# Two-stage attention and two dense layers on one Trainium2 core: a list order made at build time, weight conversion spread over the loads, and half-height matmuls in place of zero-padded ones

## Chip, cores and metric

The kernel runs on 1 core of one Trainium2 chip. The metric is the device time of one execution in microseconds (us); lower is better. The engines are named as in the profile: PE (matmul), PEld (its weight loads, which overlap PE), DVE (vector), ACT (scalar), POOL (GpSimd), SP (which only issues DMAs here).

## The reference, cut to what matters

```python
batch, n_heads, seq, head_dim = 8, 8, 576, 64        # q, k, v; p has 32 rows per head
def sm_attn(qq, kk, vv):
    a = softmax(qq @ kk.T / 8)                         # with the row maximum taken off
    return a @ vv
p_packed = sm_attn(p, k, v)                            # 32 x 64 per head
attn = sm_attn(q, p_packed, p_packed)                  # 576 x 64 per head
x = attn as [4608, 512]
h = x @ w_in1                                          # [4608, 2048]
g = (a0 + a1 h + a2 h^2 + a3 h^3) / (1 + |b0| |h| + |b1| h^2 + 1e-6)
x = g @ w_out1                                         # [4608, 512]
h = x @ w_in2
out = (h * cos(h)) @ w_out2
```

The four weight matrices come as 64-bit floats and are turned into 32-bit ones on the chip from their two 32-bit words.

## The kernel before

**Attention.** A unit is one batch with four of its eight heads: 16 units. For each unit SP loads p, k, q and v (`load`), PE transposes p, k and q, PE computes the packed scores (`scores`, 0), DVE and ACT do their softmax, PE transposes the exponentials (`turn_exp`), and `pack` multiplies them with v: 6 column blocks of 96 rows times 4 heads, 24 matmuls. The packed rows are transposed (`turned`, `by_parity`), stored to DRAM (`keep_pack`) and used for the second scores. The second softmax runs on DVE, POOL and ACT (`turn2` to `turn_back`), and its 32x576 per head go to DRAM (`keep_attn`).

A head has only 64 contraction rows. `by_parity` writes each head's 64 rows into a 128-row operand whose other 64 rows are zero, and one matmul always uses all 128 rows of the array. `m_load` and `m_prod` (line 249) do the same for the first layer: the attention output of a batch is a product of the second softmax with packed rows, so `m_prod` multiplies the packed rows with `w_in1` first. A batch needs 8 such products, each [128, 512] from 4 matmuls of 32 output rows; `m_hi` (ACT, L259) and `m_lo` (DVE, L263) split each into two 32-bit parts of lower precision, whose sum is the value. There are 64 products in all.

**First layer.** 16 half batches of 288 rows times 8 pairs of 128 hidden columns make 128 items. An item is a `front` (L326, 12 matmuls of 288 columns into a PSUM tile `h`), an epilogue, and a `back` (L363, 24 matmuls of 288 columns, which add onto four accumulators). The epilogue has on ACT `absolute`, `lin`, `slope`, `rsqrt`, `square`, `upper`; on POOL `denom` (L437); on DVE `cubic` twice (L423, L425, they read `h` in PSUM) and four steps whose operands all lie in SBUF: `over` twice (L447), `ratio` (L451), `lower` (L479, which makes `gl`).

**Second layer.** 9 chunks of 512 rows times 16 column blocks make 144 items with a `front` (L342) and a `back` (L363) of 12 matmuls each, 512 columns wide.

**Weights.** A tile of 128x512 64-bit values is loaded (`w_load`), ACT makes two parts (`w_exp` L131, `w_low` L136), DVE joins them (`w_abs` L146, `w_join` L163), and `w_split` or `keep_hi`/`keep_lo` split the result (ACT, POOL). There are 64 tiles, 16 for each matrix, and two landing buffers (`raw`).

**Order.** Each engine runs its instructions in the order in which the program issues them. That order is written out by hand: every step has a time in units of items (`plan`, `plan1`, `plan2`, `begins`, `starts`, `weight_steps`, `MOVED`), and the steps are issued sorted by it. In the first layer it has a fixed period:

```python
plan1 = (
    (0.000, front), (0.437, absolute), (0.583, lin), (0.620, slope), (0.626, cubic, 0), (0.735, denom),
    (0.882, cubic, 1), (1.753, rsqrt), (1.895, square), (2.041, over, 1), (2.097, over, 0), (2.388, ratio),
    (3.033, upper), (3.268, lower), (4.074, back, 2), (4.275, back, 1), (4.724, back, 3), (4.790, back, 0),
)
```

## Time and profile before

| what | value |
|---|---|
| median of 3 runs (range) | 1717.53 us (1717.34 to 1721.29) |
| the profiled execution, its own time | 1716.86 us |
| its span, first to last instruction | 1715.1 us |
| PE, DVE, ACT, POOL busy | 1622.7, 1371.0, 1072.2, 347.0 us |
| mean granted clock of PE | 0.983 of 2.4 GHz |
| moved by DMA | 120.77 MB |

A busy time is the sum of the stretches in which an engine runs something. An engine that is busy for almost all of a stage bounds it; the stages here have different bounds, so the tables below go by stage.

### The profile page before, as it was taken

What the parts mean: (1) busy time and instruction counts of PE and PEld (TensorE: products, weight loads), DVE (VectorE), ACT (ScalarE), POOL (GpSimd) and SP (SyncE); (2) the same over time, 40 slices, a digit from 0 to 9 for tenths busy, and PEclk for the clock granted to TensorE, in tenths of its full rate; (3) what the DMA queues carried; (4) which work ended last, traced back from release to release, by engine and by line L of the source; (5) the groups of instructions that cost most, each with busy time, mean ns of one, the idle gap of its engine ahead of it and who ended that gap; (6) DMA issues with size and microseconds to landing.
All of it is one profiled execution on the core that took longest, in us unless ns stands there. A gap on an engine that the chain in (4) does not pass through costs nothing.

```text
span 1715.1 us, 26803 instructions
## 1 busy us (share of the span) xinstructions
PE 1622.7 (95%) x10272; PEld 1354.7 (79%) x10272; DVE 1371.0 (80%) x2057; ACT 1072.2 (63%) x1770; POOL 347.0 (20%) x252
## 2 busy tenths in 40 slices
PE   5877779999999999999999999999999999999997
PEld 3554668989898988898998778888888888888886
DVE  4678999999999999999999976666676667666765
ACT  6766888888898888888886643434333333343432
POOL 1334543424343433333322200000000000000000
PEclk9888889999999999999999999999999999999999
DMA  9998321111211121111353210101010101010001
GB/s 293 273 264 249 111 83 54 48 51 49 71 49 46 49 71 49 47 37 34 117 182 101 86 44 7 44 7 44 6 38 13 37 13 37 13 33 17 22 4 25
DMA packets 78881, 120.77 MB, mean 70 GB/s; under 512 B 14752, under 2 KB 54688, under 8 KB 78752
## 3 DMA queue, kind: packets, MB, share of 16 engines
q1 hardware_dynamic: 78752, 119.05, 23.7%
q8 instruction: 81, 1.33, 0.3%
q14 instruction: 48, 0.39, 0.1%
HBM read 85.99 MB, written 33.03 MB: 69 GB/s over the span
## 4 chain that ended last, share of the span: by engine, by line
PE 73%; DVE 11%; DMA 6%; ACT 5%; issue 4%; SPq 0%; POOL 0%; DVEq 0%; ACTq 0%
PE acc L363 38%; PE h L342 21%; PE h L326 9%; DMA raw<-in_moe_w_in_dram 3%; PE m L249 3%; DMA raw<-in_moe_w_out_dram 2%; DVE T L447 2%; DVE T L451 2%; DVE gl L479 1%; DVE Q L447 1%; DVE w L163 1%; DVE w L146 1%; DVE T L423 1%; ACT g L131 1%; ACT w L136 1%
## 5 line engine op out<-in xcount | busy, mean ns | idle before, releaser
L363 PE MATMUL acc<-gh,wo 128*128 128x288 f32 x2048 | 419.9, 299 | 0.0
L363 PEld LDWEIGHTS acc<-gh,wo 128*128 128x128 f32 x2048 | 328.6, 188 | 50.5 <-issue 20.0
L363 PE MATMUL acc<-wo,gh 128*128 128x512 f32 x1152 | 359.5, 393 | 0.0
L363 PE MATMUL acc<-gl,wo 128*128 128x288 f32 x1024 | 303.2, 296 | 1.0 <-DVE gl L479 1.0
L437 POOL TENSOR_TENSOR Q<-Q,V 128x576 f32<-128x576 f32 x128 | 199.2, 1556 | 402.8 <-ACT Q L431 287.4
L463 ACT ACTIVATE Y<-Y,cst 128x512 f32<-128x512 f32 x144 | 104.4, 725 | 253.8 <-DVE Y L459 253.8
L363 PEld LDWEIGHTS acc<-wo,gh 128*128 128x128 f32 x1152 | 216.3, 188 | 49.8
L326 PE MATMUL h<-a2h,m 128*128 128x288 f32 x1024 | 230.9, 301 | 21.9 <-DVE m L263 18.0
L363 PE MATMUL acc<-wo,gl 128*128 128x512 f32 x576 | 228.1, 396 | 1.8 <-DVE gl L479 1.8
L416 ACT ACTIVATE T<-h,cst 128x512 f32<-128x512 f32 x144 | 99.2, 689 | 201.8 <-PE h L342 201.8
L456 DVE TENSOR_SCALAR T<-T 128x512 f32<-128x512 f32 x144 | 62.5, 434 | 192.4 <-ACT T L416 192.4
L326 PEld LDWEIGHTS h<-a2h,m 128*128 128x128 f32 x1024 | 174.8, 192 | 31.5 <-DVE m L263 27.2
L363 PEld LDWEIGHTS acc<-gl,wo 128*128 128x128 f32 x1024 | 192.6, 188 | 1.7 <-DVE gl L479 1.5
L326 PE MATMUL h<-a2l,m 128*128 128x288 f32 x512 | 153.0, 299 | 0.0
L342 PE MATMUL h<-x,m 128*128 128x512 f32 x576 | 145.7, 395 | 0.0
L342 PE MATMUL h<-x,win 128*128 128x512 f32 x576 | 145.6, 395 | 0.0
L363 PEld LDWEIGHTS acc<-wo,gl 128*128 128x128 f32 x576 | 108.1, 188 | 30.0 <-DVE gl L479 5.1
L342 PEld LDWEIGHTS h<-x,win 128*128 128x128 f32 x576 | 108.1, 188 | 25.9
L342 PEld LDWEIGHTS h<-x,m 128*128 128x128 f32 x576 | 108.1, 188 | 25.9
L447 DVE SCALAR_TENSOR_TENSOR Q<-Q,V 128x576 f32<-128x576 f32 x128 | 99.8, 779 | 32.1 <-ACT V L443 31.8
L466 DVE TENSOR_TENSOR G<-Y,h 128x512 f32<-128x512 f32 x144 | 98.8, 686 | 30.6 <-ACT Y L463 30.6
L428 ACT ACTIVATE V<-h 128x576 f32<-128x576 f32 x128 | 83.4, 651 | 60.0 <-PE h L326 58.7
(99 smaller groups left out, 2954.8 us busy)
## 6 DMA issues: line engine op xcount, KB each, us to landing
raw<-in_moe_w_in_dram SPq DMA_DIRECT2D x32, 512.0 KB, 4.3
raw<-in_moe_w_out_dram SPq DMA_DIRECT2D x32, 512.0 KB, 3.6
k_in<-in_k_dram SPq DMA_DIRECT2D x16, 576.0 KB, 8.2
q_in<-in_q_dram SPq DMA_DIRECT2D x16, 576.0 KB, 7.5
v_in<-in_v_dram SPq DMA_DIRECT2D x48, 192.0 KB, 7.8
x<-ob SPq DMA_DIRECT2D x16, 576.0 KB, 4.1
out_dram<-ob SPq DMA_DIRECT2D x144, 64.0 KB, 1.7
a<-a2T SPq DMA_DIRECT2D x16, 288.0 KB, 4.8
```

The costliest lines, as they stand in the source:

```text
L249: nc.tensor.matmul(ps[r, :], lhsT=PT[g][:, h % 2, r], rhs=WIN1[2 * g + h // 2, half][:, o : o + CH], start=True, stop=True,)
L326: nc.tensor.matmul(ps[:, e, 0:HS], lhsT=w[:, o : o + P], rhs=x[:, g, :], start=n == 0, stop=n == 3 * NG - 1,)
L342: nc.tensor.matmul(h, lhsT=w[:, ks], rhs=x, start=n == 0, stop=n == 3 * KC - 1)
L363: nc.tensor.matmul(o, lhsT=w, rhs=x, start=i == 0 and n == 0, stop=i == last and n == len(todo) - 1,)
L416: nc.scalar.activation(T, hidden(j), AF.Identity, scale=1.0 / (2 * PI), bias=cst[:, 1:2])
L428: nc.scalar.activation(new(j, "V", 3), hidden(j), AF.Abs)
L437: nc.gpsimd.tensor_tensor(Q, Q, V, op=ALU.mult)
L447: nc.vector.scalar_tensor_tensor(t, t, add, E[j]["V"], op0=ALU.add, op1=ALU.mult)
L451: nc.vector.scalar_tensor_tensor(T, E[j]["Q"], 2.0, T, op0=ALU.subtract, op1=ALU.mult)
L456: nc.vector.tensor_scalar(T, T, MAGIC, MAGIC, op0=ALU.add, op1=ALU.subtract)
L463: nc.scalar.activation(Y, Y, AF.Sin, bias=cst[:, 2:3])
L466: nc.vector.tensor_tensor(new(j, "G", 3), E[j]["Y"], hidden(j), op=ALU.mult)
```

## The change

The steps are the same computation, with these edits:

- **Order.** A class `Plan` takes every step with its engine, an estimated duration, what it reads and writes, the buffers that it needs, and a key. `order()` is a list scheduler: it keeps a clock for each engine, and of the steps that an engine could start within 60 ns of its first it takes the one with the smallest key. Buffers are named one by one and handed out in this order. Keys are the item's nominal place plus a number for each kind of step from a table (`WANTED`, about a hundred numbers).
- **The lock.** POOL's steps and those of DVE that have all operands in SBUF share one more clock, `port`, so that in the planned order no two of them overlap. Nothing of this is in the program: no semaphore or wait is added for it.
- **Weights.** `w_in1` tiles are now two loads of 64 rows each, and eight of them, like eight of `w_out1`, come after the attention loads have been issued.
- **Half-height matmuls.** `m_prod` and `scores` use 64 contraction rows per matmul, heads of even and odd number in the upper and lower half of the array; the zero-padded operands and `by_parity` are gone. `m_prod` writes two PSUM banks at once, 8 matmuls; there are 32 of them, and `m_hi`, `m_lo` take 1024 columns each.
- **v.** v lies in 128 partitions (four loads of 32 partitions with 1 KB runs, two more with 256-byte runs), and `pack` has 5 blocks times 4 heads, 20 matmuls.

```diff
-    def m_prod(b, qt, g, k):
-        ps = MPS[b, qt, g] = banks2(k, "m")[:, 0, :]
-        half, o = divmod(qt * CH, SLAB)
-        for h in range(G4):
-            r = slice(h * NP, (h + 1) * NP)
-            nc.tensor.matmul(
-                ps[r, :],
-                lhsT=PT[g][:, h % 2, r],
-                rhs=WIN1[2 * g + h // 2, half][:, o : o + CH],
+    def m_prod(b, a, g):
+        for e in range(2):
+            rows = slice(e * D, (e + 1) * D)
+            for h in range(G4):
+                r = slice(h * NP, (h + 1) * NP)
+                k2, o = divmod(a * H + g * G4 + h, 2)
+                nc.tensor.matmul(
+                    TILE["mps", b, a, g][r, e, :],
+                    lhsT=TILE["PT", b, g][rows, r],
+                    rhs=TILE["win1", k2][rows, o * DM : (o + 1) * DM],
...
         if (l, which) == (0, "i"):
-            kk, n = divmod(f, FF // DM)
-            nc.sync.dma_start(r64, w_in1[kk * P : (kk + 1) * P, n * DM : (n + 1) * DM])
+            a, h = divmod(f, H)
+            for e in range(2):
+                n = 2 * a + e
+                nc.sync.dma_start(
+                    r64[e * D : (e + 1) * D, :], w_in1[h * D : (h + 1) * D, n * DM : (n + 1) * DM]
+                )
...
-            d[nm] = ld.tile([TP, G4, TCN, D], F32, tag=nm, name="v_in")
-            rows = v[b, hs].rearrange("h (p j c) d -> j p h c d", j=NJ, c=TCN)
-            for j in range(NJ):
-                nc.sync.dma_start(d[nm][32 * j : 32 * (j + 1)], rows[j])
+            rows = v[b, hs].rearrange("h (p c) d -> p h c d", c=2 * NT9)
+            for j in range(4):
+                nc.sync.dma_start(t[32 * j : 32 * (j + 1), :, 0:4, :], rows[:, :, 4 * j : 4 * j + 4, :])
+            for e in range(2):
+                nc.sync.dma_start(t[32 * e : 32 * (e + 1), :, 4, :], rows[:, :, 16 + e, :])
...
+    SHARED = ("over", "ratio", "lower", "rounded", "clipped", "w_abs", "w_join", "x_lo")
...
+        s.port = eng == "POOL" or fn.__name__ in self.SHARED or (fn.__name__ == "reduced" and args[1] == 1)
...
+        def may(s):
+            t = max(free[s.eng], s.ready)
+            if s.port:
+                t = max(t, free["port"])
...
-    for _, _, fn, a in sorted(todo, key=lambda x: x[:2]):
-        fn(*a)
+    for s in plan.order():
+        for _, o, shape, dt in s.new:
+            make(o, s.slots[o], shape, dt)
+        s.fn(*s.args)
```

What this moves is seen in the order of the instructions. **First place: the DMAs that SP issues first.** Before (L112 loads a weight tile, L515 p, L527 k or q):

```order
L112 DMA raw<-in_moe_w_in_dram 128x512 x2
L515 DMA p_in<-in_p_dram 128x64 x2
L527 DMA k_in<-in_k_dram 128x1152
L515 DMA p_in<-in_p_dram 128x64
L527 DMA k_in<-in_k_dram 128x1152
L515 DMA p_in<-in_p_dram 128x64
L112 DMA raw<-in_moe_w_in_dram 128x512
L527 DMA q_in<-in_q_dram 128x1152
```

With the change (L341 a weight tile, L439 p, L451 k or q, L445 and L447 v):

```order
L341 DMA raw_160<-in_moe_w_in_dram 64x512 x2
L341 DMA raw_163<-in_moe_w_in_dram 64x512 x2
L439 DMA p_in_166<-in_p_dram 128x64
L439 DMA p_in_168<-in_p_dram 128x64
L439 DMA p_in_170<-in_p_dram 128x64
L451 DMA q_in_172<-in_q_dram 128x1152
L451 DMA q_in_174<-in_q_dram 128x1152
L451 DMA q_in_176<-in_q_dram 128x1152
L445 DMA v_in_178<-in_v_dram 32x4x256 x4
L447 DMA v_in_178<-in_v_dram 32x4x64 x2
```

Three units' q and v now stand ahead of the first k (which is ten rows further down). Up to DVE's first `cubic`, 23 weight tiles have been joined before and 19 with the change; in the twelve items after it, 9 and 13.

**Second place: DVE in the middle of the first layer.** Before (L423 and L425 `cubic`, L447 `over`, L479 `lower`, L451 `ratio`, L263 `m_lo`):

```order
L263 TENSOR_TENSOR m<-m 128x512
L423 TENSOR_TENSOR T<-T,h 128x576
L425 SCALAR_TENSOR_TENSOR T<-T,par,h 128x576
L447 SCALAR_TENSOR_TENSOR Q<-Q,V 128x576
L447 SCALAR_TENSOR_TENSOR T<-T,par,V 128x576
L479 TENSOR_TENSOR gl<-T,gh 128x576
L451 SCALAR_TENSOR_TENSOR T<-Q,T 128x576
L423 TENSOR_TENSOR T<-T,h 128x576
```

With the change (L850 and L852 `cubic`, L875 `over`, L879 `ratio`, L910 `lower`):

```order
L850 TENSOR_TENSOR T_9244<-T_9244,b_1_9210 128x576
L852 SCALAR_TENSOR_TENSOR T_9244<-T_9244,par,b_1_9210 128x576
L850 TENSOR_TENSOR T_9289<-T_9289,b_0_9228 128x576
L852 SCALAR_TENSOR_TENSOR T_9289<-T_9289,par,b_0_9228 128x576
L910 TENSOR_TENSOR gl_9344<-T_9080,gh_9276 128x576
L879 SCALAR_TENSOR_TENSOR T_9130<-U_9111,T_9130 128x576
L875 SCALAR_TENSOR_TENSOR U_9247<-U_9247,V_9241 128x576
L875 SCALAR_TENSOR_TENSOR T_9244<-T_9244,par,V_9241 128x576
L875 SCALAR_TENSOR_TENSOR U_9279<-U_9279,V_9257 128x576
L879 SCALAR_TENSOR_TENSOR T_9244<-U_9247,T_9244 128x576
```

The fixed period of one item is gone; here two items' `cubic` steps, which read PSUM, stand together, and the steps that lie in SBUF follow. On PE the same shows as two fronts in a row, at 39 places of the first layer, often followed by 48 or more matmuls of `back`; before, 12 matmuls of `front` and 24 of `back` alternate throughout.

**Third place: PE at a product.** Before (L326 `front`, L249 `m_prod`, L363 `back`):

```order
L326 MATMUL h<-a2h,m 128x288
L249 MATMUL m<-win_179,pt_154 32x512 x2
L249 MATMUL m<-win_188,pt_154 32x512 x2
L363 MATMUL acc<-gh,wo 128x288 x2
L363 MATMUL acc<-gl,wo 128x288
```

With the change (L739 `front`, L694 `m_prod`, L776 `back`):

```order
L739 MATMUL b_0_5352<-a_0_4879,m01l 128x288
L694 MATMUL b_1_5375<-s_2447,pt_4452 32x512 x2
L694 MATMUL b_1_5375<-s_2520,pt_4452 32x512 x2
L694 MATMUL b_1_5375<-s_2447,pt_4452 32x512 x2
L694 MATMUL b_1_5375<-s_2520,pt_4452 32x512 x2
L776 MATMUL acc_5165<-gh_5257,wo_2142 128x288 x2
```

A product has 8 matmuls instead of 4, and there are half as many products.

## Rows read from the trace of the kernel before

**Rows 1.** Busy time by stage; columns as in the first line (x: instructions)

```profile
core 0: us, PE busy (x) PEld busy (x) DVE busy (x) ACT busy (x) POOL busy (x), PEclk, DMA share, GB/s
0.00:164.00 164.00, 117.72 (x1712) 75.86 (x1712) 108.49 (x215) 114.89 (x246) 50.42 (x63) 0.92 0.98 272
164.00:250.00 86.00, 63.95 (x397) 52.37 (x398) 82.48 (x101) 69.47 (x110) 44.89 (x29) 0.84 0.34 108
250.00:850.00 600.00, 586.68 (x4328) 527.84 (x4327) 567.16 (x736) 515.43 (x820) 213.62 (x138) 1.00 0.17 56
850.00:888.00 38.00, 38.00 (x287) 38.00 (x287) 35.01 (x50) 34.37 (x56) 11.12 (x8) 1.00 0.54 169
888.00:1010.00 122.00, 120.05 (x552) 97.36 (x551) 112.03 (x166) 75.18 (x124) 26.92 (x17) 1.00 0.30 90
1010.00:1695.00 685.00, 685.00 (x2957) 554.74 (x2956) 458.69 (x782) 258.40 (x411) 0.00 (x0) 1.00 0.09 22
1695.00:1716.00 21.00, 11.27 (x48) 8.56 (x46) 7.14 (x12) 4.43 (x7) 0.00 (x0) 0.88 0.21 51
```

**Rows 2.** DMA of 60 to 100 us: one GB/s figure per microsecond

```profile
GB/s 361 187 197 226 218 246 297 404 391 318 183 206 229 204 240 311 404 398 249 214 241 206 214 265 325 369 403 252 224 301 233 267 369 282 346 267 313 243 197 195
...
v_in<-in_v_dram SPq DMA_DIRECT2D x13, 192.0 KB, 7.8
```

**Rows 3.** Chain of waits, 20 to 164 us: start us, us, what

```profile
24.82 9.76 DMA k_in<-in_k_dram
35.10 9.85 DMA raw<-in_moe_w_in_dram
...
127.89 8.36 DMA raw<-in_moe_w_out_dram
```

**Rows 4.** Timeline of PE before the first front: start us, us, instruction [idle before, releaser]

```profile
155.80 0.88 PE L638 MATMUL pp<-v_in,e1T 96*32 96x64 f32 x48 [1.39 <-DMA v_in<-in_v_dram]
...
164.35 0.61 PE L326 MATMUL h<-a2h,m 128*128 128x288 f32 x1 [0.98 <-DVE m L263]
```

**Rows 5.** Timeline of PE, 24 matmuls of back and the next front

```profile
600.34 0.43 PE L363 MATMUL acc<-gh,wo 128*128 128x288 f32 x2
...
603.54 0.29 PE L326 MATMUL h<-a2h,m 128*128 128x288 f32 x1
```

**Rows 6.** Timeline of PE at a product

```profile
612.10 0.29 PE L326 MATMUL h<-a2h,m 128*128 128x288 f32 x1
612.32 0.16 PEld L249 LDWEIGHTS m<-win,pt 128*32 128x32 f32 x8 [0.17 <-issue]
612.32 1.06 PE L249 MATMUL m<-win,pt 128*32 128x512 f32 x8
...
613.32 0.54 PE L363 MATMUL acc<-gh,wo 128*128 128x288 f32 x2
```

**Rows 7.** Busy time by stage of line 249 alone (PE, PEld)

```profile
164.00:250.00 86.00, 10.24 (x56) 1.31 (x56) 0.84 0.34 108
250.00:850.00 600.00, 58.59 (x440) 8.95 (x440) 1.00 0.17 56
```

**Rows 8.** Timeline of DVE and POOL in the first layer

```profile
599.91 0.75 DVE L447 SCALAR_TENSOR_TENSOR Q<-Q,V 128x576 f32<-128x576 f32 x1
600.58 0.81 DVE L447 SCALAR_TENSOR_TENSOR T<-T,par,V 128x576 f32<-128x576 f32 x1
601.31 0.75 DVE L479 TENSOR_TENSOR gl<-T,gh 128x576 fp32r<-128x576 f32 x1
601.98 0.75 DVE L451 SCALAR_TENSOR_TENSOR T<-Q,T 128x576 f32<-128x576 f32 x1
...
605.37 0.68 DVE L163 SCALAR_TENSOR_TENSOR w<-raw,w 128x512 uint32<-128x512 uint32 x1
...
606.83 1.77 POOL L178 TENSOR_TENSOR lo<-w,hi 128x512 fp32r<-128x512 f32 x1 [2.65 <-issue]
...
607.37 1.84 DVE L479 TENSOR_TENSOR gl<-T,gh 128x576 fp32r<-128x576 f32 x1
```

**Rows 9.** Groups of DVE instructions by form: count, busy us, mean ns, idle before

```profile
L447 DVE SCALAR_TENSOR_TENSOR T<-T,par,V 128x576 f32<-128x576 f32 x128 | 117.9, 921 | 0.0
L479 DVE TENSOR_TENSOR gl<-T,gh 128x576 fp32r<-128x576 f32 x128 | 112.9, 882 | 0.0
L451 DVE SCALAR_TENSOR_TENSOR T<-Q,T 128x576 f32<-128x576 f32 x128 | 112.0, 875 | 0.0
L447 DVE SCALAR_TENSOR_TENSOR Q<-Q,V 128x576 f32<-128x576 f32 x128 | 99.8, 779 | 32.1 <-ACT V L443 31.8 <-issue 0.2
```

**Rows 10.** Busy time by stage of line 163 alone (DVE)

```profile
164.00:250.00 86.00, 12.27 (x10) 0.84 0.34 108
```

**Rows 11.** Waits, whole span: who for whom, total us, times, longest us

```profile
PEld h L326 <- DVE m L263: 27.2, 21, 5.6
```

More of the change, by code (lines that the diff above doesn't have):

```diff
@@ L68, in pack_attention_moe_moe_kernel @@
     EARLY = 8
[L70 to L73 removed]
+    N1 = NH * NPR
+    NI = N1 + NCH * NF
     POOL = {}
[L76 to L80 removed]
@@ new lines, in pack_attention_moe_moe_kernel, with make, dram @@
+    SLOTS["tr"] = ["b2_0", "b2_1", "b3"]
+    plan = Plan(SLOTS, ("tr", "b2", "one", "raw", "sc", "xr"))
+    add = plan.add
+    TILE = {}
+    def make(o, slot, shape, dt):
+        TILE[o] = POOL[HOME[slot]].tile(shape, dt, tag=slot, name=slot)
+    def dram(nm, n, shape):
+        return [POOL["dp"].tile(shape, F32, name=f"{nm}_{i}") for i in range(n)]
+    a2 = dram("a2", NU, [P, S])
+    ppt = dram("ppt", NU, [P, P])
+    x2 = dram("x2", NH, [DM, HS])
+    w2 = dram("w2", NF, [P, 2 * DM])
@@ new lines, in pack, with packed @@
+    def pack(u):
+        for c in range(5):
+            for h in range(G4):
+                r, ks = slice(h * NP, (h + 1) * NP), slice(0, D if c == 4 else P)
+                nc.tensor.matmul(
+                    TILE["ppp", u][r, 0:D],
+                    lhsT=TILE["e1T", u][ks, c, r],
+                    rhs=TILE["v", u][ks, h, c, :],
+                    start=c == 0,
+                    stop=c == 4,
+                )
+    def packed(u):
+        nc.vector.tensor_scalar(
+            TILE["pp", u],
+            TILE["ppp", u][:, 0:D].unsqueeze(1).to_broadcast([P, 2, D]),
+            TILE["sm", u][:, 3:4],
+            None,
+            op0=ALU.mult,
+        )
@@ new lines, in m_hi, with m_lo, layer, win2_of @@
+    def m_hi(b, a, g):
+        nc.scalar.copy(TILE["M", b, a, g, "h"], flat2(TILE["mps", b, a, g]))
+    def m_lo(b, a, g):
+        hi, lo = (TILE["M", b, a, g, e] for e in "hl")
+        nc.vector.tensor_tensor(lo, flat2(TILE["mps", b, a, g]), hi.bitcast(F32), op=ALU.subtract)
+    items = [(0, c, i) for c in range(NH) for i in range(NPR)]
+    items += [(1, c, f) for c in range(NCH) for f in range(NF)]
+    def layer(j):
+        return items[j][0]
+    def win2_of(f):
+        return halves_of(TILE["win2", f])
@@ new lines, in open_right @@
+    def open_right():
+        actx.close()
+        pctx.close()
+        opened("aps", space=PSUM, reuse_waits="tile")
+        for nm in ("gp", "op", "xp", "wo1"):
+            opened(nm, side="right", reuse_waits="tile")
+    for u in range(NU):
+        attention(u)
+    OPEN["sl2"] = OPEN["a2p"] = OPEN["ep"] = add("-", 0, 0, open_left, after=ld_users)
+    t = add("-", 0, 0, open_right, after=tp_users)
+    OPEN |= dict.fromkeys(("gp", "op", "xp", "wo1", "aps"), t)
+    for n in range(0, NF, NF // 2):
+        for e, which in enumerate("io"):
+            for f in range(n, n + NF // 2):
+                convert(0, f, which, -612.8 + 6.86 * (f + n + e * NF // 2))
@@ new lines, in pack_attention_moe_moe_kernel @@
+    KEEP1, KEEPN = 14, 6.2
+    for c in range(NH):
+        operands1(c)
+        for i in range(NPR):
+            j = c * NPR + i
+            item1(j)
+            for f in range(NF):
+                if j == int(KEEP1 + KEEPN * f):
+                    convert(1, f, "i", at(j + 3), after=[fronts[j]])
+    for f in range(NF):
+        add("SP", 60, at(N1 - 9 + f / 2), w_back, f, r=[("w2", f)], new=[(HOMES2[f], ("win2", f), [P, 2 * CH], F32R)], kb=512)
+    operands2(0)
+    for f in range(NF):
+        n = max(N1 - 2, N1 - 4 + f)
+        convert(1, f, "o", at(N1 + f), after=[fronts[min(n, N1 - 1)]])
```

1236 lines of the change are left out of this document (622 added, 614 removed), and 10 rows, old and new, of tables (WANTED, begins).

## Prediction

> **What bounds the kernel now.** I read the busy time by stage first [rows 1]. It shows four parts with different limits.
>
> From 0 to 164 us PE, DVE and ACT are each busy for about two thirds, while the DMA share is 0.98 at 272 GB/s. The chain of waits through this stretch steps from one load of 8 to 10 us to the next [rows 3], and the last pieces of v still hold PE up at 155.8 us, 8.6 us before the first front at 164.35 [rows 4]. So DMA bounds the attention.
>
> From 164 to 250 us DVE is busy for 82.5 of 86 us: it is the ramp of the first layer, where weight tiles are still being joined.
>
> From 250 to 850 us PE is busy for 586.7 of 600 us and DVE for 567.2. What does PE need there? It has 4328 matmul records, and 440 of them belong to the products [rows 7], 8 to each, so 55 products; the other 3888 are 108 items of 36. The 24 matmuls of a back take from 600.34 to 603.54, 3.20 us or 0.133 us each [rows 5], so an item needs 36 x 0.133 = 4.80 us. A product holds PE from the start of the last matmul of a front to the next back, 612.10 to 613.32, 1.22 us [rows 6]. Together 108 x 4.80 + 55 x 1.22 = 518 + 67 = 585 us. PE is the bound, 15 us of the stretch are waits, and DVE is close behind.
>
> From 1010 to 1695 us PE is busy all the time at full clock: 2957 matmuls in 685 us, 0.2317 us each, 24 to an item [rows 1].
>
> A profiled execution took 1716.86 us, 0.7 us under the median; the sum is made against it. A difference within 0.3% (5 us) can't be told from no change.
>
> **The products.** There will be 32 instead of 64, about 27.5 instead of 55 between 250 and 850 us. What one costs is not in the trace, since no matmul there uses half of the array's rows. If the halves run side by side, a product of 8 matmuls takes the 1.22 us that one of 4 takes now; if they run one after the other, the 1.00 us from its first matmul to the next back [rows 6] comes twice, 2.22 us. I take 1.22. Four matmuls of 32 columns already overlap: they have 8 records, and 8 passes of 512 columns at 0.2317 us would need 1.85 us, where the row shows 1.00. So PE needs 33.5 us less (27.5 x 1.22), or only 6 us less (67.1 - 27.5 x 2.22 = 6.0) at the other end. The 7 products of the ramp are worth nothing, as DVE bounds it.
>
> **The lock.** Does DVE fit into 600 - 34 = 566 us, when it is busy for 567? Its four steps in SBUF take 0.75, 0.81, 0.75 and 0.75 us undisturbed, 3.06 together [rows 8], but 0.779 + 0.921 + 0.882 + 0.875 = 3.46 us on average [rows 9]. The difference is POOL: the `lower` that begins at 607.37, while POOL runs from 606.83 to 608.60, takes 1.84 us, which is 1.23 us until POOL is done and 0.61 us of work [rows 8]. That makes 0.40 us an item, 43 us in this stretch, so DVE has 524 us of work of its own. The new order keeps such steps apart in the plan, but nothing holds them apart on the chip, and the engines will drift. I take half of the 43 us as saved: 546 us, which fits. None saved would leave DVE at 567 us plus some waits; with half of today's 33 us of idle time the stretch would be 583 us. All saved, and the 15 us of PE's waits gone too, it would be 551 us. My value for the stretch is 566 us, 34 less.
>
> **The ramp.** Four more weight tiles are joined within the first twelve items. Two steps of 0.68 us each [rows 8] make 4 x 1.36 = 5.4 us more on DVE. Against that stands what POOL blocks: L163 took 12.27 us for 10 steps there [rows 10], 5.5 us over 10 x 0.68, and twelve items at 0.40 us make 4.8. Half of these 10.3 us saved is 5.2. Net 0, between -6 us and +10.
>
> **The attention stage.** The first front will need 19 tiles of weights where 23 were joined before. Four tiles of 0.524 MB less are 2.1 MB, 7.7 us at 272 GB/s [rows 1]. But 11 of the 19 are `w_in1` tiles, loaded in two halves of 64 partitions. The nearest rows are the loads of v, 32 partitions at a time: the GB/s of single microseconds lie at about 200 for stretches and near 400 in others [rows 2]. At 200 a tile takes 2.6 us, at 400 1.3 us, so 11 tiles could cost 14 us. The page "SBUF — State Buffer" of the Trainium skill, section on the DMA port swizzle, speaks against this edit: 64 partitions reach 8 of the 16 ports, about 218 GB/s where 128 reach 436. By its figures I estimate 1.2 us a tile, 13 us; the trace has the two levels, but no row here shows 64 partitions. The last load is now q instead of v: after v, 8.6 us pass through `pack`, two transposes and the second scores [rows 4]; after q only transposes, a product and its two splits remain. I give 3 us for it. Net -7.7 + 14 - 3 = +3 us, from -11 (the halves overlap) to +12 (the end is not shorter, and k, which is behind three units of q and v, starts the work later).
>
> **The rest.** The 16 x 4 fewer matmuls of `pack` and the shorter scores lie beside the loads and count nothing; without that cover the 0.88 us of a `pack` [rows 4] would give 16 x 0.15 = 2.3 us. `m_hi` and `m_lo` handle as many elements as before. From 850 to 1010 us PE is busy for 158 of 160, and from 1010 to 1695 for all of it with the same number of matmuls: 0, between -3 and +6 us if the irregular order makes PE wait. Stores at the end are the same.
>
> Sum: -34 + 0 + 3 + 0 = -31 us. **1716.9 - 31 = 1686 us.**
>
> **The rivals.**
>
> *The planned order fits better than I think.* The stretch falls to 551 us (-49), the ramp gains 6 and the attention 11: 1717 - 66 = 1651 us. For it: three engines have room once POOL no longer blocks DVE. Against: the plan's durations are fixed numbers, and DMA, which bounds the start, is a rough model. Chance 0.17.
>
> *DVE becomes the bound*, because the lock is only in the plan and does not do what its name says. The stretch takes 583 us: -17 + 3 = -14, 1703 us. For it: DVE is only 20 us behind PE now. Chance 0.13.
>
> *The halves of the array don't overlap.* Then the stretch gives 6 us and the start takes 3: 1714 us, no change that can be told. For it: no row shows two halves at work. The page "TensorEngine Tiling (Array Packing)" of the Trainium skill, section "Key Properties", says that tiles run in parallel, and its gotchas ask for different PSUM banks, which the change uses; no row here shows either. Chance 0.06.
>
> *Slower: the order is brittle.* In the first layer two fronts stand together at 39 places, and the backs behind them need the `gl` of up to three items, with two `gl` buffers. PE runs strictly in that order, so a late `lower` on DVE stops fronts too. A wait of this kind has its price in the trace: fronts waited for DVE's `m_lo` 21 times, 27.2 us in all, 1.3 us each [rows 11]. At 39 places that is 51 us, and -31 + 51 = +20: 1737 us. It turns into a loss from 31/39 = 0.8 us a place. For it: the fixed period, which suited such waits, is gone. Against: backs of older items lie between, 3.2 us each. Chance 0.12.
>
> **How the numbers follow.** The forecast, 1672 to 1700 us, has 0.52, and the rivals have 0.48. Faster by over 5 us: 0.52 + 0.17 + 0.13, and nothing of the others, 0.82. Within 5 us: the 0.06 of the halves. Slower: 0.12. The range reaches from the better plan's 1651, less 3 us for the second layer, to 1712, which leaves out the slower rival and some of the halves: 1648 to 1712 us.
>
> **What would show it.** Between the ramp and the second layer, the time from one front to the next, 600/108 = 5.56 us now, should be 5.24 us. A product should hold PE for about 1.2 us, with 32 of them; 2.2 us would show halves one after the other. The mean of DVE's `lower`, `ratio` and `over` should fall from 0.86 us towards 0.81. The first front should begin between 153 and 176 us. PE should wait for `gl` or T rarely: waits of more than 0.8 us at the pairs of fronts would make me wrong, and so would a second layer that is not 5.56 us an item.

## The result, and the profile after

The changed kernel takes 1731.2 us (median, 1729.3 to 1731.7), the kernel before 1717.4 us beside it. The ratio is 1.0073, 95% interval 1.0055 to 1.0090: **slower by 0.7%**. I had said 1686 us, 1648 to 1712.

Busy time by stage of the changed kernel, the columns of [rows 1]:

```profile
core 0: us, PE busy (x) PEld busy (x) DVE busy (x) ACT busy (x) POOL busy (x), PEclk, DMA share, GB/s
0.00:164.00 164.00, 109.65 (x1583) 69.71 (x1583) 92.04 (x195) 99.71 (x199) 47.56 (x57) 0.88 0.92 266
164.00:250.00 86.00, 61.40 (x379) 53.12 (x371) 77.37 (x103) 67.03 (x105) 37.00 (x24) 0.73 0.38 108
250.00:850.00 600.00, 561.79 (x4314) 526.44 (x4315) 581.59 (x712) 503.81 (x799) 232.91 (x141) 0.99 0.18 58
850.00:1010.00 160.00, 153.63 (x841) 134.15 (x840) 147.43 (x213) 106.54 (x179) 42.24 (x26) 0.99 0.32 100
1010.00:1695.00 685.00, 684.94 (x2957) 552.28 (x2956) 449.08 (x784) 241.71 (x414) 0.00 (x0) 1.00 0.09 23
```

From 250 to 850 us PE has given up its place: 561.8 us busy where it was 586.7 [rows 1], and DVE is now busy for 581.6 of 600. In DVE's groups, against [rows 9]:

```profile
L875 DVE SCALAR_TENSOR_TENSOR T<-T,par,V 128x576 f32<-128x576 f32 x128 | 128.4, 1003 | 0.0
L910 DVE TENSOR_TENSOR gl<-T,gh 128x576 fp32r<-128x576 f32 x128 | 127.2, 994 | 7.4 <-PE acc L776 6.4 <-ACT V L855 0.5 <-ACT gh L907 0.4
L879 DVE SCALAR_TENSOR_TENSOR T<-U,T 128x576 f32<-128x576 f32 x128 | 118.5, 926 | 0.1
L875 DVE SCALAR_TENSOR_TENSOR U<-U,V 128x576 f32<-128x576 f32 x128 | 103.3, 807 | 1.5 <-ACT V L871 1.5
```

I had expected the four steps that work in SBUF alone to become shorter. They have become longer: 3.73 us an item instead of 3.46. The timeline says by what. DVE:

```profile
606.90 1.99 DVE L879 SCALAR_TENSOR_TENSOR T<-U,T 128x576 f32<-128x576 f32 x1
...
609.54 1.41 DVE L850 TENSOR_TENSOR T<-T,b 128x576 f32<-128x576 f32 x2
610.87 1.53 DVE L852 SCALAR_TENSOR_TENSOR T<-T,par,b 128x576 f32<-128x576 f32 x2
...
615.72 0.75 DVE L879 SCALAR_TENSOR_TENSOR T<-U,T 128x576 f32<-128x576 f32 x1
...
619.97 1.98 DVE L910 TENSOR_TENSOR gl<-T,gh 128x576 fp32r<-128x576 f32 x1
```

and POOL in the same stretch:

```profile
606.53 1.75 POOL L864 TENSOR_TENSOR U<-U,V 128x576 f32<-128x576 f32 x1 [2.23 <-ACT U L858]
610.51 1.44 POOL L864 TENSOR_TENSOR U<-U,V 128x576 f32<-128x576 f32 x1 [2.23 <-ACT U L858]
617.15 2.02 POOL L864 TENSOR_TENSOR U<-U,V 128x576 f32<-128x576 f32 x1 [5.21 <-DVE gl L910]
619.80 1.53 POOL L864 TENSOR_TENSOR U<-U,V 128x576 f32<-128x576 f32 x1 [0.63 <-ACT U L858]
```

A `ratio` (L879) that begins 0.37 us after a POOL instruction takes 1.99 us, where an undisturbed one takes 0.75: it stands until POOL is done at 608.28. The same with `lower` at 619.97. At 610.51 the plan works as meant: `cubic` (L850, L852), which reads `h` in PSUM, lies beside POOL and takes its usual 0.7 to 0.8 us each. The section "Who interferes with whom" of the Trainium skill's page "SBUF — State Buffer" says so: a DVE instruction with two inputs in SBUF and a POOL instruction that reads SBUF exclude each other for a whole instruction, and the first one wins. These rows agree.

The products run as I had said. Line 694 alone, by stage, and one of them on PE's timeline:

```profile
250.00:850.00 600.00, 29.83 (x448) 6.01 (x448) 0.99 0.18 58
```

```profile
623.57 1.09 PE L694 MATMUL b<-s,pt 64*32 64x512 f32 x16 [0.71 <-issue]
624.59 0.53 PE L776 MATMUL acc<-gh,wo 128*128 128x288 f32 x2
```

Sixteen records make a product now: 28 products by 1.07 us, where 55 by 1.07 stood [rows 7]. The two halves of the array run side by side, and PE needs 28.8 us less. The 96 items of the table below become only 8.0 us shorter, because PE waits for DVE. Waits of PE and of its weight loads in the whole span, then of PE from 330 to 854 us (total us, times, longest us):

```profile
PEld b L739 <- issue: 34.1, 29, 4.0
PE b L739 <- DVE T L852: 28.6, 29, 3.5
```

```profile
PE b L739 <- DVE T L852: 19.4, 24, 2.1
PE acc L776 <- DVE gl L910: 0.8, 2, 0.5
```

A front waits until the second `cubic` has freed its buffer of `h`, 29 times, up to 3.5 us; in the middle of the layer 24 times, up to 2.1 us. A `back` hardly ever waits for `gl` there.

Where the 14.6 us of span went, by the first matmul of a front on PE's timeline: the 1st front +3.2 us (167.6 for 164.4), from there to the 25th +9.4, the 96 items to the 121st -8.0, the last 8 items up to layer 2 +5.8, layer 2 +4.2, the tail 0.

### The profile page after: what moved, and what is told of

It reads as the page before. It is cut to its first block, busy times and chain, and to the rows that moved or that the text cites. A ratio compares the mean times of both kernels' runs of the same rounds, so it can differ in the third digit from the quotient of the medians.

```text
span 1729.7 us, 26781 instructions
## 1 busy us (share of the span) xinstructions
PE 1597.8 (92%) x10176; PEld 1356.9 (78%) x10176; DVE 1361.2 (79%) x2025; ACT 1026.0 (59%) x1706; POOL 359.7 (21%) x246
## 4 chain that ended last, share of the span: by engine, by line
PE 59%; DVE 25%; ACT 6%; issue 5%; DMA 4%; SPq 1%; POOL 0%; DVEq 0%; ACTq 0%; POOLq 0%
PE acc L776 28%; PE b L755 22%; PE b L739 5%; DVE T L875 4%; DVE gl L910 4%; DVE T L879 4%; DVE T L850 3%; DVE U L875 3%; DVE T L852 2%; PE b L467 1%; PE b L694 1%; DMA k_in<-in_k_dram 1%; DVE sc L367 1%; ACT T L841 1%; DVE sc L377 1%
## 5 line engine op out<-in xcount | busy, mean ns | idle before, releaser
L776 PE MATMUL acc<-gh,wo 128*128 128x288 f32 x2048 | 423.6, 301 | 7.6 <-ACT gh L907 7.2
L776 PE MATMUL acc<-wo,gh 128*128 128x512 f32 x1152 | 359.1, 393 | 0.0
L776 PEld LDWEIGHTS acc<-gh,wo 128*128 128x128 f32 x2048 | 336.0, 192 | 29.4 <-issue 13.6
L776 PE MATMUL acc<-gl,wo 128*128 128x288 f32 x1024 | 307.5, 300 | 7.8 <-DVE gl L910 7.8
L864 POOL TENSOR_TENSOR U<-U,V 128x576 f32<-128x576 f32 x128 | 216.2, 1695 | 397.6 <-ACT U L858 327.2
L776 PEld LDWEIGHTS acc<-wo,gh 128*128 128x128 f32 x1152 | 216.1, 188 | 49.2
L776 PE MATMUL acc<-wo,gl 128*128 128x512 f32 x576 | 226.6, 393 | 0.0
L898 ACT ACTIVATE U<-U 128x512 f32<-128x512 f32 x144 | 90.8, 631 | 203.7 <-DVE U L894 203.7
L776 PEld LDWEIGHTS acc<-gl,wo 128*128 128x128 f32 x1024 | 196.5, 192 | 9.6 <-DVE gl L910 9.6
L910 DVE TENSOR_TENSOR gl<-V,gh 128x512 fp32r<-128x512 f32 x144 | 100.4, 697 | 131.1 <-PE acc L776 127.3
L910 DVE TENSOR_TENSOR gl<-T,gh 128x576 fp32r<-128x576 f32 x128 | 127.2, 994 | 7.4 <-PE acc L776 6.4
L875 DVE SCALAR_TENSOR_TENSOR T<-T,par,V 128x576 f32<-128x576 f32 x128 | 128.4, 1003 | 0.0
L776 PEld LDWEIGHTS acc<-wo,gl 128*128 128x128 f32 x576 | 108.1, 188 | 25.0 <-DVE gl L910 0.2
L883 DVE TENSOR_SCALAR T<-T 128x512 f32<-128x512 f32 x144 | 63.5, 441 | 80.3 <-ACT T L843 80.1
L879 DVE SCALAR_TENSOR_TENSOR T<-U,T 128x576 f32<-128x576 f32 x128 | 118.5, 926 | 0.1
L841 ACT ACTIVATE T<-b,par 128x576 f32<-128x576 f32 x128 | 106.4, 833 | 19.3 <-DVE gl L910 18.1
L858 ACT ACTIVATE U<-V,par 128x576 f32<-128x576 f32 x128 | 110.5, 870 | 0.1
L901 DVE TENSOR_TENSOR V<-U,b 128x512 f32<-128x512 f32 x144 | 98.4, 683 | 15.1 <-ACT U L898 10.7
L890 DVE SCALAR_TENSOR_TENSOR U<-T,U 128x512 f32<-128x512 f32 x144 | 102.5, 712 | 4.2
```

What stands on the lines that cost most here:

```text
L776: nc.tensor.matmul(o, lhsT=w, rhs=x, start=i == 0 and n == 0, stop=i == last and n == len(todo) - 1,)
L841: nc.scalar.activation(T, hidden(j), AF.Identity, scale=par[:, 3:4], bias=par[:, 2:3])
L858: nc.scalar.activation(shaped(j, "U"), shaped(j, "V"), AF.Identity, scale=par[:, 5:6], bias=par[:, 4:5])
L864: nc.gpsimd.tensor_tensor(Q, Q, V, op=ALU.mult)
L875: nc.vector.scalar_tensor_tensor(t, t, add_, shaped(j, "V"), op0=ALU.add, op1=ALU.mult)
L879: nc.vector.scalar_tensor_tensor(T, shaped(j, "U"), 2.0, T, op0=ALU.subtract, op1=ALU.mult)
```

## The experiments

All runs but the four of the single transfer stand in one table. "Front 1, 25, 121" and "layer 2" are the starts of those fronts. "Item" is the mean time between the 25th and the 121st front. "Steps" is the mean of DVE's `over` (both), `ratio` and `lower` in it, undisturbed 0.77 us. "Blocked" is what all DVE instructions there took above the undisturbed time of their form. These columns are read from the profiled execution of each kernel, whose time lies within 6 us of the median (a_square 1685.5, b_square 1700.9).

| kernel | median us | ratio to before [95%] | front 1, 25, 121, layer 2 (us) | item | steps | blocked |
|---|---|---|---|---|---|---|
| before | 1717.4 | 1 | 164.4, 315.9, 849.7, 888.0 | 5.56 | 0.868 | 51.6 |
| changed | 1731.2 | 1.007 [1.006, 1.009] | 167.6, 328.5, 854.3, 898.4 | 5.48 | 0.929 | 68.7 |
| a_square | 1691.3 | 0.984 [0.982, 0.987] | 163.9, 316.4, 816.8, 854.6 | 5.21 | 0.826 | 20.6 |
| b_square | 1696.8 | 0.987 [0.985, 0.990] | 168.1, 315.4, 833.6, 871.9 | 5.40 | 0.845 | 26.7 |
| a_split | 1707.9 | 0.995 [0.993, 0.996] | 170.5, 325.0, 834.8, 876.5 | 5.31 | 0.891 | 53.6 |
| b_split | 1706.7 | 0.994 [0.992, 0.996] | 165.7, 315.9, 842.3, 880.7 | 5.48 | 0.869 | 44.2 |
| a_nolock | 1757.2 | 1.023 [1.021, 1.025] | 171.4, 330.0, 875.0, 918.8 | 5.68 | 0.960 | 80.3 |
| a_unpair | 1756.8 | 1.023 [1.020, 1.026] | 169.1, 330.6, 883.7, 929.8 | 5.76 | 0.886 | 52.0 |
| b_halves | 1777.1 | 1.034 [1.031, 1.037] | 184.1, 342.3, 899.6, 944.9 | 5.80 | 0.954 | 84.6 |
| b_pieces | 1735.3 | 1.010 [1.007, 1.013] | 181.9, 333.8, 868.5, 906.9 | 5.57 | 0.869 | 52.3 |
| a_conv | 1760.6 | 1.025 [1.023, 1.027] | 178.0, 357.1, 882.3, 926.3 | 5.47 | 0.923 | 65.4 |
| a_kfirst | 1725.6 | 1.004 [1.003, 1.006] | 171.8, 334.8, 854.5, 898.4 | 5.41 | 0.905 | 59.6 |
| a_raw3 | 1728.0 | 1.007 [1.005, 1.008] | 188.1, 331.6, 856.9, 898.2 | 5.47 | 0.902 | 58.2 |
| a_square_k | 1693.4 | 0.986 [0.984, 0.988] | 170.1, 327.0, 825.9, 865.3 | 5.20 | 0.816 | 16.6 |
| a_square_split | 1686.4 | 0.982 [0.980, 0.985] | 170.4, 321.3, 818.1, 855.9 | 5.17 | 0.822 | 19.1 |
| a_square_re | 1679.5 | 0.978 [0.976, 0.981] | 167.5, 312.6, 806.8, 847.1 | 5.15 | 0.813 | 14.6 |

### POOL's product taken away: a_square, b_square

My theory after the result, D: DVE bounds layer 1, because POOL's `denom` blocks its steps. The rival, O: the order makes PE wait, whatever DVE's steps take. The edit lets ACT's `slope` do both steps, |b1| h² + |b0| |h| = (s|h| + t)² - t². In both kernels alike:

```diff
-            shaped(j, "U"), shaped(j, "V"), AF.Identity, scale=par[:, 5:6], bias=par[:, 4:5]
+            shaped(j, "U"), shaped(j, "V"), AF.Square, scale=par[:, 5:6], bias=par[:, 4:5]
...
-        nc.gpsimd.tensor_tensor(Q, Q, V, op=ALU.mult)
+        pass
```

Columns 4 to 6 of `par` hold t, s and 1 + 1e-6 - t²; the last is the bias of `rsqrt` and the addend of `over`.

> The changed kernel in its own order, but POOL's product in layer 1 is gone: ACT forms |b1| h^2 + |b0| |h| by one squaring of s|h| + t (s the root of |b1|, t = |b0| / 2s), and the later bias takes -t^2. The result stays the reference's, and POOL does nothing between. Theory D (DVE bounds layer 1, because POOL blocks its steps in SBUF): the four steps fall from 0.93 us on average to about 0.77, DVE needs 0.65 us an item less, PE becomes the bound at 4.80 + 0.31 = 5.1 us an item, and the run falls by 35 to 50 us, to 1681 to 1696 us. Theory O (the order itself makes PE wait, whatever DVE's steps take): less than 10 us, 1721 to 1731 us, with the waits at the first front of a group still there.

> The kernel before, with the same squaring in place of POOL's product. Theory D: PE bounds layer 1 here (586.7 us of 600), so that only its 15 us of waits and some of the ramp can be won: 5 to 20 us, 1697 to 1712 us, less than half of what the changed kernel wins. Theory O gives no difference between the two kernels here: 0 to 10 us in both.

D holds. The changed kernel gains 40 us and the kernel before 21. Busy time of a_square, and of b_square, from 250 to 850 us:

```profile
250.00:850.00 600.00, 586.75 (x4564) 557.39 (x4557) 566.22 (x756) 540.67 (x849) 49.13 (x29) 1.00 0.20 66
```

```profile
250.00:850.00 600.00, 599.50 (x4450) 543.64 (x4450) 562.59 (x757) 528.41 (x840) 55.92 (x29) 1.00 0.18 58
```

In b_square PE rests for 0.5 of 600 us, and an item takes 5.40 us, the 4.80 of its matmuls and half a product of 1.22: there PE, with the old products, is the bound. In a_square the item is 5.21 us, close to the 5.24 I had predicted for the change itself. The waits of its fronts have fallen, from 34.1 and 28.6 us to:

```profile
PEld b L739 <- issue: 15.0, 14, 4.0
PE b L739 <- DVE T L852: 10.1, 9, 3.1
```

The changed kernel's gain lies where D had it; the other is just past the upper end of D's 5 to 20 us and a little over half as large, not under it. Taking `denom` away also takes a step out of the chain from `slope` to `rsqrt`, so these two runs alone can't tell a relieved DVE from a shorter chain. The next two, which keep the step, can. Outside the 96 items the edit takes back what the change had lost: the ramp from the first to the 25th front falls from 160.9 to 152.5 us (151.5 in the kernel before), the last 8 items from 44.1 to 37.8 (38.3). The steps stay at 0.83 and not 0.77: `over` takes its addend from `par` now (0.81 us undisturbed, 0.75 with a constant), and 18 of them still took over 1 us beside POOL's other work.

### POOL's product in two pieces: a_split, b_split

```diff
-        nc.gpsimd.tensor_tensor(Q, Q, V, op=ALU.mult)
+        for e in range(2):
+            nc.gpsimd.tensor_tensor(Q[:, e], Q[:, e], V[:, e], op=ALU.mult)
```

> The changed kernel with POOL's product in layer 1 issued as two instructions of half the elements. Theory L (a step of DVE in SBUF waits until the POOL instruction that runs has ended, 1.70 us here): the longest waits are halved, DVE's four steps fall from 0.93 us on average to 0.83 to 0.88, the time by 10 to 30 us, to 1701 to 1721 us. Rival (the two engines wait as long in sum, in more pieces): the four steps stay above 0.90 us, the time within 6 us of the changed kernel's or above.

> The kernel before with POOL's product in two instructions. Theory L: DVE's steps get shorter here as well, but PE bounds layer 1, so no more than the 20 us that taking the product away gave: 1700 to 1716 us. Rival: within 5 us of the kernel before, or above.

`denom` in the changed kernel and in a_split (count | busy us, mean ns), and two of DVE's steps beside POOL in a_split:

```profile
L864 POOL TENSOR_TENSOR U<-U,V 128x576 f32<-128x576 f32 x128 | 216.2, 1695 | 397.6 <-ACT U L858 327.2 <-DVE T L879 23.2 <-DVE T L850 21.6
L865 POOL TENSOR_TENSOR U<-U,V 128x288 f32<-128x288 f32 x256 | 261.5, 1046 | 341.0 <-ACT U L858 214.3 <-issue 69.2 <-DVE T L880 20.7
```

```profile
618.97 2.10 POOL L865 TENSOR_TENSOR U<-U,V 128x288 f32<-128x288 f32 x2
619.25 1.14 DVE L911 TENSOR_TENSOR gl<-T,gh 128x576 fp32r<-128x576 f32 x1
620.32 1.37 DVE L880 SCALAR_TENSOR_TENSOR T<-U,T 128x576 f32<-128x576 f32 x1
```

The same work in two instructions gives the changed kernel 23 us and the kernel before 11. The times are as theory L has them, the steps not quite: 0.891 us in a_split, just above its 0.83 to 0.88, and unchanged in b_split, where the joins of weights gained instead. `Blocked` fell by 15 and 7 us, and the 96 items by 16 and 7. In the 96 items of a_split 75 of the 384 steps took over 1 us, at 1.40 us on average, where in the changed kernel 59 did, at 1.83. So DVE waits more often but for less time, and in sum for less, although `denom` keeps POOL busy for longer (261.5 us for 216.2). The chain from `slope` to `rsqrt` has not become shorter here; DVE's blocked time has.

### The lock and the order: a_nolock, a_unpair

```diff
-        s.port = eng == "POOL" or fn.__name__ in self.SHARED or (fn.__name__ == "reduced" and args[1] == 1)
+        s.port = False
```

> The changed kernel, but the plan that sets its order has no lock between POOL and DVE's steps in SBUF. Theory D (the lock is only in the plan, and the engines drift apart from it on the chip): DVE's four steps still take 0.90 to 0.96 us on average, and the time is within 6 us of the changed kernel's, 1725 to 1737 us. Rival (the lock does keep many of the steps apart): the four steps take over 1.0 us on average, and the time is 15 us or more above the changed kernel's.

My theory missed on the time: an order planned without the lock is 26 us slower. The lock doesn't hold on the chip, but an order planned with it blocks DVE for 68.7 us in the 96 items, and one without it for 80.3. The rival's time came, its size of the steps (over 1.0) did not; 0.960 is the upper end of my theory's. The 96 items are 19 us longer, the blocked time 12; what makes up the rest I didn't look into.

```diff
-        ... "front 0": -113 ...
+        ... "front 0": 0 ...
```

> The changed kernel with the rank of a layer-1 front no longer 113 us ahead of its own time (one number changed: -113 to 0), so that older backs go first. Theory O (fronts that stand together make PE wait): layer 1 gets 10 us or more shorter, below 1722 us. Theory D (DVE bounds layer 1; the place of the fronts only has to give DVE its work early): no gain, and a loss where DVE runs out of work: 1728 to 1790 us.

With fronts at their own time the run is 26 us longer, though DVE is blocked less. Busy time of a_unpair, and of the changed kernel:

```profile
330.00:590.00 260.00, 234.05 (x1772) 216.05 (x1770) 234.01 (x291) 206.84 (x330) 89.95 (x58) 0.98 0.15 48
330.00:590.00 260.00, 243.05 (x1871) 228.08 (x1871) 251.56 (x309) 218.07 (x346) 99.72 (x60) 0.99 0.17 53
```

DVE is idle for 26 of 260 us here, for 8 in the changed kernel: theory D's loss. But the edit did not do what its name says. On PE's timeline fronts of layer 1 stand together at 44 places of a_unpair, up to four in a row; in the changed kernel at 41, always two. So the run tests how early the fronts rank, not the pairs.

The slower rival of the prediction falls by other rows. a_square has the same 41 pairs and is 40 us faster. And in the changed kernel the backs hardly wait for `gl` (0.8 us in all from 330 to 854 us, above); the fronts wait for `cubic`, and nearly always the first one of a pair or a single one. Whether an order with fewer pairs would be faster or slower is not shown: a_nolock (10 groups) and a_square_re below (15) have fewer, but differ in much else.

### The new products in the old order, and the loads: b_halves, b_pieces

b_halves is the kernel before with the new `m_prod`, its products at four places for each batch of the old table, where eight stood, and `w_in1` laid out and loaded as in the change. b_pieces has nothing but the loads in two pieces:

```diff
-            nc.sync.dma_start(r64, w_in1[kk * P : (kk + 1) * P, n * DM : (n + 1) * DM])
+            for e in range(2):
+                r = kk * P + e * D
+                nc.sync.dma_start(r64[e * D : (e + 1) * D, :], w_in1[r : r + D, n * DM : (n + 1) * DM])
```

> The kernel before in its own order, with one part of the change: 32 products of 8 matmuls in halves of the array in place of 64 of 4 (and w_in1 loaded in two pieces of 64 partitions). My prediction's term was 33.5 us less on PE, which would be 1684 us if nothing else bounds it. Theory D: PE needs 27 to 33 us less, but DVE with its blocked steps, busy for 567 of 600 us, gives only 10 to 20 us of it: 1697 to 1707 us. Theory O (the new products are as good as predicted, and only the new order spoils them): 25 to 35 us less, 1682 to 1692 us. If the pieces of 64 partitions delay the start, the first front is later than 164 us by up to 14 us.

> The kernel before with one edit: each tile of w_in1 is loaded in two pieces of 64 partitions instead of one of 128. Theory P (a load of half the partitions moves at half the rate, and DMA bounds the attention): 16 tiles by 1.2 to 1.3 us put the first front 15 to 22 us later than 164 us, and the time at 1730 to 1740 us. Rival (the two pieces overlap): the first front within 4 us of 164 us, the time within 6 us of the kernel before. With theory P the 60 us that the kernel before lost with the new products are in part the loads, not the products.

b_halves missed both theories, 60 us slower than before. b_pieces, which came as theory P had it, explains 18 of them: the first front moves from 164.4 to 181.9 us and nothing later makes up for it, 1.1 us a tile. DMA of b_pieces from 25 to 65 us:

```profile
DMA packets 4503, 9.89 MB, mean 247 GB/s; under 512 B 1111, under 2 KB 2847, under 8 KB 4497
```

and of the kernel before:

```profile
DMA packets 5380, 11.55 MB, mean 289 GB/s; under 512 B 1252, under 2 KB 3517, under 8 KB 5373
```

The prediction had taken 1.3 us a tile. The Trainium skill's "SBUF — State Buffer", section on the port swizzle, from which I estimated 1.2 us, agrees. The other 42 us of b_halves, by the profiled executions against b_pieces: 2 at the first front, 23 in the 96 items, at 5.80 us each with DVE blocked for 84.6, and 6, 7 and 5 in the ramp, before layer 2 and in it. So the new product at these four places of an order made for the old one is a loss. Which of its places cause it I have not tried.

### One transfer in place of two: a_one, b_halves_one, a_square_one, a_square_one_k

```diff
-            for e in range(2):
-                n = 2 * a + e
-                nc.sync.dma_start(
-                    r64[e * D : (e + 1) * D, :], w_in1[h * D : (h + 1) * D, n * DM : (n + 1) * DM]
-                )
+            nc.sync.dma_start(
+                r64,
+                w_in1[h * D : (h + 1) * D, 2 * a * DM : 2 * (a + 1) * DM].rearrange("d (e c) -> e d c", e=2),
+            )
```

> The changed kernel with each w_in1 tile loaded by one transfer over 128 partitions (both column blocks of a head's 64 rows) instead of two over 64. Theory P (two pieces cost 17.5 us for 16 tiles in the kernel before, 1.1 us a tile, and ten tiles lie ahead of the first front here): the first front 7 to 12 us earlier than 167.6 us, the time 1719 to 1726 us. Rival (the start waits for k, not for bytes): the first front within 4 us of 167.6 us, the time within 5 us of the changed kernel's.

> The kernel before with the 32 products in halves of the array, and w_in1 in one transfer a tile. If the loads were 17 us of that kernel's loss and the rest lies in the order (24 products that hold a buffer of two banks for twice as long, in an order with a fixed place for each), the first front is at 163 to 170 us and the time 1756 to 1763 us, still 40 us above the kernel before, with 5.8 us an item. If the loads spoilt the later stages too, it is below 1735 us.

> The squaring in place of POOL's product and the single transfers together, in the order of the changed kernel: if both causes are apart, their gains add, 40 us and 5 to 12 us, 1679 to 1687 us. If DVE or the ramp takes the earlier start back, 1688 to 1694 us.

> As the run before, with the loads of k ranked first, which alone gave 6 us, though not at the first front: 1673 to 1682 us if that gain adds too, 1682 to 1690 us if it was the place of DVE's steps against POOL's that happened to be better.

All four missed, and by far: 1846.9, 1908.1, 1808.0 and 1800.3 us (ratios 1.076, 1.111, 1.053 and 1.049). In a_one the first front begins at 242.9 us. Its stages at a `w_in1` load:

```profile
64.00:72.00 8.00, 1.95 (x13) 1.22 (x17) 1.58 (x3) 2.94 (x6) 0.00 (x0) 0.50 0.14 53
```

While such a transfer runs, with a slowest dimension of 2 (the two column blocks), the DMA share is 0.14 at 53 GB/s; two of 16 engines would be 0.125. The Trainium skill has the rule in "DMA: Bandwidth & Descriptors", section "Why a DMA increments its semaphore by 16 and not by 1": the number of engines must divide the slowest dimension of both sides. I had overlooked it. What two pieces cost the changed kernel itself these runs therefore don't tell. They tell one thing: behind the late start the items take 5.45, 5.83, 5.20 and 5.20 us, within 0.03 of the changed kernel, b_halves, a_square and a_square_k. So the loads spoil the start, and what b_halves loses in its items is not theirs.

### The ramp: a_conv, a_kfirst, a_raw3, a_square_k

a_conv converts all `w_in1` tiles before the `w_out1` tiles; a_kfirst sets `"load k"` from 168 to -168; a_raw3 gives the raw tiles a third buffer (and, in an edit not shown, ties `w_low` to the conversion before it, so that the order of the tiles stays):

```diff
-        ("raw", "st", ("raw0", "raw1")),
+        ("raw", "st", ("raw0", "raw1", "raw2")),
```

> The changed kernel with all 16 w_in1 tiles converted before the first w_out1 tile (it takes eight of one and eight of the other by turns). Theory R (its fourth pause, 23.5 us between the 4th and the 5th front, stands there because the second eight w_in1 tiles come last): the 5th front at 185 us or earlier (206.7 now), the 25th at 315 to 322 us (328.5), the run 6 to 13 us shorter, 1718 to 1725 us. Rival (DVE bounds the ramp, whatever the order of its tiles): the 25th front within 4 us of 328 us and the time within 5 us of the changed kernel's.

> The changed kernel with the loads of k ranked before those of q and v (one number of the table changed: +168 to -168). Theory K (the work starts late since k stands behind three units of q and v): the first front 4 to 10 us earlier than 167.6 us, and the run by as much shorter, 1721 to 1727 us. Rival (the bytes bound the stretch, in whatever order): the first front within 3 us of 167.6, the time within 5 us.

> The changed kernel with three buffers for raw weight tiles instead of two (and a rule that keeps the conversions in their order). Theory B (the conversions during the loads are held up by the two buffers, each waiting for a transfer behind q, k and v, so that only 15 of 32 are joined before the first front, 23 in the kernel before): 18 or more joined tiles at the first front, the 25th front 6 to 15 us earlier than 328.5 us, the time 1716 to 1725 us. Rival (DMA is full, and a weight tile that comes earlier puts off a tile of q, k or v): the first front later by as much as the ramp gets shorter, the time within 5 us of the changed kernel's or above it.

> The squaring in place of POOL's product, with the loads of k ranked first, in the changed kernel: the two gains alone are 40 and 6 us. If both stand, 1683 to 1688 us, the best time of all; if the 6 us came from the place of DVE's steps against POOL's product, 1689 to 1694 us.

In the changed kernel 23.5 us lie between the 4th and the 5th front. In a_conv, where the `w_in1` tiles come first, 7.0 us do, so theory R had a cause of this pause, but not its worth: the first front is 10 us later (178.0 for 167.6), the 5th at 199.0 and not by 185, and the 25th at 357.1. Its waits come at other places: from 165 to 360 us PE waits 31 us for `cubic` at fronts and products, in the changed kernel 11. Why was not followed.

In a_raw3 25 tiles are joined at the first front (16 in the changed kernel, counted on DVE's timeline), the pause is 3.9 us, and the ramp from the 1st to the 25th front takes 143.5 us instead of 160.9, as theory B had it. But the first front is 20 us later, and the 25th 3 us later than in the changed kernel, as the rival said.

a_kfirst doesn't put the first front earlier (171.8), its pause is 33.4 us, and it gains its 6 us in the 96 items, where DVE is blocked for 59.6 us instead of 68.7; without POOL's product the same edit gives nothing (a_square_k).

So none of these edits brings the 25th front forward by more than 2 us. At that front 33 or 34 tiles are joined in every kernel of the table, however many of them were joined before the first (15 to 25; 22 in the kernel before): what is not loaded and joined ahead of the first front is made up for in the ramp.

### The best version: a_square_split, a_square_re

a_square_split has POOL's other subtractions (`w_lo`, `a2_lo`) in two instructions each; a_square_re takes `denom` out of the plan too, so that the list is made again:

```diff
-        add("POOL", 1390, key, denom, j, r=[("V", j)], w=[("U", j)])
```

> The kernel with the squaring in the changed kernel's order, and POOL's other long steps (the low parts of the weights and of the attention, 1.4 to 1.7 us each) in two instructions. What POOL still takes from DVE between the 25th and the 121st front is 20.6 us there; theory L: half of that goes, 1680 to 1687 us. Rival (these waits are beside others by now, and PE is as near to its bound as DVE): within 5 us of 1691 us.

> The kernel with the squaring, and the list planned again without POOL's product, so that DVE's steps no longer keep clear of an instruction that isn't there: 1680 to 1688 us if the free places are of use to DVE; if the order was well enough, within 5 us of 1691 us; a loss of 10 us or more would show that the order is sensitive to every length in it.

The pieces give 5 us, which can't be told from nothing, and `blocked` fell by 1.5 us, not by half. The new list is 12 us faster than a_square by the medians, 7 by the profiled executions: **1679.5 us, 2.2% below the kernel before**. Its busy time:

```profile
164.00:250.00 86.00, 59.87 (x403) 50.22 (x395) 77.66 (x108) 71.53 (x113) 25.62 (x17) 0.80 0.37 108
250.00:850.00 600.00, 595.46 (x4625) 563.14 (x4624) 572.43 (x770) 550.15 (x860) 51.33 (x29) 1.00 0.21 69
```

PE is busy for 595.5 of 600 us: it bounds the layer again, with the new products.

## Why the prediction was wrong

Between the forecast of -31 us and the +14.6 of the span lie 45.6 us: 26 in the stretch (-34 said, -8.0 in the 96 items), 9.4 in the ramp, 10.0 in the rest.

*The bound.* Right for the kernel before: with DVE relieved PE is busy for 599.5 of 600 us (b_square).

*The products.* Right in the mechanism, a little high in size: 1.07 us for twice the work, 28.8 us less on PE, where 33.5 were said. The 1.22 us read from [rows 6] begin with the last matmul of a front, whose 0.13 us the 36 matmuls of the item hold already. The rival of halves that don't overlap is out, and "Key Properties" of the Trainium skill's "TensorEngine Tiling (Array Packing)", that tiles run in parallel, agrees with the trace.

*The lock.* **This is the step that failed: "I take half of the 43 us as saved: 546 us, which fits."** Nothing was saved. From the 25th to the 121st front DVE was blocked for 68.7 us instead of 51.6, and it became the bound at 5.48 us an item, not 5.24. Taking POOL's product away brings 5.21, and the 96 items become 33.4 us shorter than in the kernel before, about as much as I had said of the change alone. I had seen that the lock is in the plan only, and that an undisturbed 3.06 us stands against 3.46, but bounded the blocked time by today's value, as if it could only fall. The plan's lock does help (26 us, a_nolock). By count the new order blocks more since the two engines meet more often: in the 96 items 59 of the 384 steps took over 1 us (1.83 on average), where 34 did in the kernel before (1.92) and 90 without the lock (1.58). So the fixed period of the old order kept them apart better than the plan does. Where the plan's clocks part from the chip's was not followed.

*The ramp.* 0 predicted, +9.4 came, inside its bounds. Of that 8.4 goes with POOL's product (a_square). The 19 and 23 joined tiles of the working are those up to DVE's first `cubic`, which comes 10 us after the first front in the changed kernel and 6 us after it in the kernel before; at the first front itself 16 are joined, where 22 were. A pause of the fronts that I had not named lies in the ramp, from 183.2 to 206.7 us, on PE's timeline:

```profile
188.61 1.50 PE L694 MATMUL b<-s,pt 64*32 64x512 f32 x16 [2.53 <-DVE T L852]
196.26 0.85 PE L776 MATMUL acc<-gh,wo 128*128 128x288 f32 x2 [6.14 <-ACT gh L907]
...
199.43 0.44 PE L776 MATMUL acc<-gl,wo 128*128 128x288 f32 x1
...
206.71 0.43 PE L739 MATMUL b<-a,m10h 128*128 128x288 f32 x2
```

The 5th front needs `m10`, whose `w_in1` tiles are converted after eight `w_out1` tiles; with the tiles in the other order the pause is 7.0 us (a_conv).

*The attention.* +3 predicted, +3.2 measured. That they agree is in part luck. Of three terms one was tested: the 1.3 us for a tile in two pieces was 1.1 in b_pieces. And kernels that are alike up to the first front have it at 163.9 to 170.5 us (changed, a_square, a_split) and at 164.4 to 168.1 (before, b_square, b_split), so that one execution each doesn't resolve 3 us. How the term splits in the changed kernel was not shown.

*The rest.* 0 predicted, -3 to +6; +10.0 came, outside these bounds: 5.8 in the last 8 items of layer 1 and 4.2 in layer 2. Of the 5.8, two waits of fronts for `cubic` are 4.2, and they go with POOL's product (these items take 37.8 us in a_square, 38.3 in the kernel before). Of the 4.2 about half remains there: from the first front of layer 2 to the end 829.1 us, 831.3 in the changed kernel, 827.1 in the kernel before. I didn't isolate that.

*The rivals.* "DVE becomes the bound" was the mechanism, with a chance of 0.13 and a price too low by 28 us: it kept the blocked time as it was (9 us), and left out the ramp (9) and the rest (10). The slower rival had about the right time (1737 us) by luck, for a wrong reason: PE doesn't wait for `gl` behind the pairs but for `cubic` ahead of them, and with the same pairs a_square is 40 us faster. The sign that I had named for being wrong came all the same, by its other half: waits for T of more than 0.8 us.

## What to carry to other kernels

Where two engines exclude each other, bound the blocked time of a new order above today's value as well, and when the engine that suffers is within a few per cent of the bound, look first for a way to take the other engine's instruction away or cut it in two: that was worth 40 and 23 us here, and of a saving of 29 us on the engine next to it the stretch kept 8 until then. Try a new product in the order that it will have: at four places of an order made for the old one it cost 42 us, beside 18 for its loads. A list that is planned from durations is worth planning again after an edit that changes them (12 us here). And look in the trace whether an edit of a key did what it is named for: a_unpair did not.
